# Winograd convolution with batch norm: storing the transformed input point by point, splitting the last pair's copies, and moving the first weights forward

## The chip, the cores and the metric

The kernel runs on one core of one Trainium2 chip. The metric is device time in microseconds of one execution, taken as the median of several runs. Beside it stands one profiled execution, whose trace gives the start and the duration of every instruction on TensorE (PE; its weight loads are PEld), VectorE (DVE), ScalarE (ACT), GpSimd (POOL) and SyncE (SP, which here issues most of the DMAs).

## The reference

```python
# x (2, 2048, 1024), w (3, 1024, 1024), mean, var, g, b (1024,), all bfloat16
xp = jnp.pad(x, ((0, 0), (1, 1), (0, 0)))
y = sum(jnp.einsum('bsc,cd->bsd', xp[:, k:k + S, :], w[k]) for k in range(3))
y = (y - mean) * (g / jnp.sqrt(var + 1e-5)) + b
return silu(y)
```

It is a convolution of three taps along the sequence, over 1024 channels in and out, followed by batch norm with given statistics and SiLU.

## The kernel before, in words

The convolution is done in the Winograd manner: six output rows (R = 6) at a time are made from eight "points" (NJ = 8). The input is transformed to eight points, the weights are transformed to eight points, the two are multiplied point by point, and the eight products are combined into six output rows. A sequence of 2048 rows gives NB = 342 groups of six.

**Input transform.** The rows of a batch are loaded in 17 overlapping windows: 16 of 128 rows (256 KB, 21 groups each) and a last one of 33 rows (6 groups). `load_x` (L125) issues each on SP's queue, into 12 rotating buffers. A matrix `rm` (128 rows by 8 points by 21 groups, built on VectorE, L79 to L104) does the transform: for each of eight channel tiles, one matmul (L278) with a piece of the window as the stationary operand and `rm` as the moving one writes 168 columns into PSUM. Window 0 uses a shifted copy of the matrix, `rm0`, made by `first_matrix`. Windows are taken in pairs, and a pair is done in three jobs (`t_jobs`, `t_job`): a has channel tiles 0 to 2, b has 3 to 5, c has 6 and 7. A job has its matmuls for the first window of the pair, then for the second, into two neighbouring PSUM banks, and is then copied in one instruction to `T_sb` in SBUF, as bf16: 1008 values per partition for a and b, 672 for c. The 33-row window is one job of 384 values. `T_sb` lies as channel tile, point, group.

Each copy goes to ScalarE (L289) or VectorE (L291). The choice is made when the program is built: `ends` and `busy` keep a rough clock for both engines, and a copy is given to the one that would finish first. Once built, the order on every engine is fixed.

**Weights.** The first weights (128 output channels of w, three chunks of 256 KB, one for each tap) are loaded between the windows; `W0_AT` says after which. `prepare_first` makes six of their eight points: `even_part` and `transform_w` run on GpSimd (L169, L179, L190), and use two multiples of taps that ScalarE makes, four times tap 2 (L175) and twice tap 1 (`double_w`, L157). Points 0 and 7 are taps as loaded.

**Products.** A `Unit` is one batch by 128 output channels, in four PSUM banks. `product` makes eight matmuls (L324) of 342 columns, one per channel tile. Products come for points 1, 3, 2, 4, 5, 6, and later 7 and 0. Points 1 and 2 are summed in bank 3 of the unit, points 3 and 4 in bank 0, points 5 and 6 in bank 2. Copies of the intermediate sums go to ScalarE (`copy`, L335 and L337), and the combinations to VectorE (`combine`, L342). After the third product (point 2), ScalarE copies bank 3 into `sd[:, 0]`, and VectorE makes `sd[:, 1]` of bank 3 and an earlier copy; this is called the sd copy and the sd pass below. The rows end in SiLU on ScalarE (L347).

**What is laid into what.** All jobs of batch 0 run first (`ahead`), in PSUM banks 0 to 7. The 25 jobs of batch 1, numbered 0 (the 33-row window) to 24 below, are laid between the matmuls of the first unit: `Between` is called after every matmul of a product, and issues jobs so that jobs 0 to 22 are spread over the first 32 matmuls (products of points 1, 3, 2 and 4). They use the bank pairs 4-5, 6-7 and 1-2 in turn, so a job waits for the copy of the job three before it. The product of point 5 then takes bank 2, and has to wait for the copy of job 20. Jobs 23 and 24 follow that product. After that there are only products, to the end.

Of the kernel before, what the change touches and what calls it, by code (L numbers as in the profile page):

```python
# [15 lines left out]
P = 128  # L16
R = 6
NJ = 8
W0_AT = (5, 8, 11)
W0_USE = 16  # L20
EARLY = 23
XBUFS = 12
WARM = 6
WT = 21

@with_exitstack
def kernel(
# [51 lines left out]
    def transform_matrix():  # L79
        v = nc.vector  # L80
        val = consts.tile([P, 3, WT], I32, name="val")
        nc.gpsimd.iota(val, pattern=[[1, 3], [-R, WT]], base=-1, channel_multiplier=1)
        m = consts.tile([P, 4, 3, WT], FP32, name="m")
        f = consts.tile([P, 3, 2, WT], FP32, name="f")
        c = consts.tile([P, 2, WT], FP32, name="c")
        rm = consts.tile([P, NJ, WT], BF16, name="rm")
        m0, m2, m4, m6 = (m[:, q] for q in range(4))
        for q, coef in ((1, -8.0), (2, 1.0), (3, 1.0), (0, 36.0)):
            v.tensor_scalar(m[:, q], val, float(2 * q), coef, op0=ALU.is_equal, op1=ALU.mult)
        for k, (c4, c6) in enumerate(((34.0, -8.0), (40.0, -32.0), (10.0, -2.0))):  # L90
            v.scalar_tensor_tensor(out=f[:, k], in0=m4[:, 1:3], scalar=c4, in1=m2[:, 1:3], op0=ALU.mult, op1=ALU.add)
        v.scalar_tensor_tensor(out=c, in0=m6[:, 0:2], scalar=-36.0, in1=m0[:, 0:2], op0=ALU.mult, op1=ALU.add)
        for k, (c4, c6) in enumerate(((34.0, -8.0), (40.0, -32.0), (10.0, -2.0))):
            v.scalar_tensor_tensor(out=f[:, k], in0=m6[:, 1:3], scalar=c6, in1=f[:, k], op0=ALU.mult, op1=ALU.add)
        v.scalar_tensor_tensor(out=c, in0=m4[:, 0:2], scalar=189.0, in1=c, op0=ALU.mult, op1=ALU.add)
        f1, f2, f3 = (f[:, k] for k in range(3))
        for j, a0, s0, a1, op in (
            (1, f1[:, 0], 1.0, f1[:, 1], ALU.add), (2, f1[:, 0], 1.0, f1[:, 1], ALU.subtract),
            (3, f2[:, 1], 2.0, f2[:, 0], ALU.add), (4, f2[:, 1], -2.0, f2[:, 0], ALU.add),
            (5, f3[:, 0], 2.0, f3[:, 1], ALU.add), (6, f3[:, 0], 2.0, f3[:, 1], ALU.subtract),  # L100
            (0, m2[:, 1], 23.625, c[:, 1], ALU.add), (7, m2[:, 0], -23.625, c[:, 0], ALU.subtract),
        ):
            v.scalar_tensor_tensor(out=rm[:, j], in0=a0, scalar=s0, in1=a1, op0=ALU.mult, op1=op)
        return rm  # L104

    rm = transform_matrix()
# [8 lines left out]
    def busy(e, size):  # L115
        clock[e] = ends(e, size)

    order = [NW - 1] + list(range(2, NW - 1)) + [0, 1]
    xwin = {}

    def load_x(bi, wi):
# [38 lines left out]
            eng.tensor_scalar(t, raw[dc][:, 1], 2.0, 0.0, op0=ALU.mult, op1=ALU.add)  # L160
        double[dc] = t

    def even_part(dc, q, eng, by=None):

        w0, w2 = raw[dc][:, 0], raw[dc][:, 2]
        e = epool.tile([P, CT, P], FP32, name=f"e{q}")
        f, h = (w2, w0) if q == 1 else (w0, w2)
        if q == 0:
            eng.tensor_tensor(e, w0, w2, op=ALU.add)  # L169
        elif eng is nc.vector:  # L170
            eng.scalar_tensor_tensor(out=e, in0=f, scalar=4.0, in1=h, op0=ALU.mult, op1=ALU.add)  # L171
        else:
            t = spool.tile([P, CT, P], BF16, name="w1x2")
            if by is nc.scalar:
                by.mul(t, f, 4.0)  # L175
                busy("act", CT * P)
            else:
                by.tensor_scalar(t, f, 4.0, 0.0, op0=ALU.mult, op1=ALU.add)
            eng.tensor_tensor(e, t, h, op=ALU.add)  # L179
        if eng is nc.vector:  # L180
            busy("dve", CT * P)
        sums[dc, q] = e
# [22 lines left out]
        act_work.append(lambda: double_w(dc, nc.scalar))  # L205
        dve_work.extend((second, third))

    def prepare_first(dc):

        even_part(dc, 0, nc.gpsimd)  # L210
        transform_w(dc, 0, (0,))
        even_part(dc, 1, nc.gpsimd, nc.scalar)
# [4 lines left out]
        even_part(dc, 2, nc.gpsimd, nc.gpsimd)  # L217
        transform_w(dc, 2)

    prm = consts.tile([P, 4, DC], BF16, name="prm")  # L220
# [7 lines left out]

    def first_matrix():

        v = ps[0:P - 1, 1, 256:256 + NJ * WT]
        nc.tensor.matmul(v, lhsT=ident[:, 1:P], rhs=rm.rearrange("p j n -> p (j n)"), start=True, stop=True)
        nc.scalar.copy(rm0[0:P - 1].rearrange("p j n -> p (j n)"), v)

    def params():

        v = ps[:, 1].bitcast(BF16)[:, 0:4 * DC]
# [15 lines left out]
    def t_jobs(bi):  # L253


        i = 0
        while i < NW:
            two = order[i:i + 2] if order[i] < NW - 1 else order[i:i + 1]
            i += len(two)
            n = LAST if two[0] == NW - 1 else WT  # L260
            wins = [
                (*xwin[bi, wi], rm if wi else rm0, min(P, S - (R * WT * wi - 1)) if wi else P - 1) for wi in two
            ]
            c0 = 0
            while c0 < CT:
                nct = min(512 // (NJ * n), CT - c0)
                yield wins, T_sb[bi][:, c0:c0 + nct, :, two[0] * WT:two[0] * WT + len(two) * n], n, c0, nct
                c0 += nct

    def t_job(job, bank):  # L270
        wins, dst, n, c0, nct = job
        nb, size = len(wins), nct * NJ * n
        clock["pe"] = max(clock["pe"], wins[-1][1], bank_free.get(bank, 0.0))
        src = ps[:, bank:bank + nb, 0:size]
        v = src.rearrange("p b (c j n) -> p b c j n", j=NJ, n=n)
        for q, (xw, _, mat, rows) in enumerate(wins):
            for c in range(nct):
                nc.tensor.matmul(  # L278
                    v[:, q, c], lhsT=xw[0:rows, (c0 + c) * P:(c0 + c + 1) * P], rhs=mat[0:rows, :, 0:n],
                    start=True, stop=True,  # L280
                )
        dst = dst.rearrange("p c j (b n) -> p (c j) b n", b=nb)
        src = src.rearrange("p b (q n) -> p q b n", n=n)
        clock["pe"] += nb * size / 2.3
        e = min(("act", "dve"), key=lambda k: ends(k, nb * size))
        busy(e, nb * size)
        bank_free[bank] = clock[e] + 100.0
        if e == "act":
            nc.scalar.copy(dst, src)  # L289
        else:  # L290
            nc.vector.tensor_copy(dst, src)  # L291

    NK = -(-NB // P)
    NBP = NK * P
# [5 lines left out]
    class Unit:  # L300
# [15 lines left out]
        def product(self, q, j, add, between):  # L316
            dc = self.dc
            nsl = slice(self.lo, self.hi)
            for ct in range(CT):
                if j == 0 or j == NJ - 1:  # L320
                    lhsT = raw[dc][:, 0 if j == 0 else 2, ct]
                else:
                    lhsT = wts[dc, (j - 1) // 2][:, (j - 1) % 2, ct]
                nc.tensor.matmul(  # L324
                    self.bank[q], lhsT=lhsT, rhs=T_sb[self.bi][:, ct, j, nsl],
                    start=not add and ct == 0, stop=ct == CT - 1, skip_group_check=add,
                )
                clock["pe"] += (self.hi - self.lo) / 2.35
                between()
# [149 lines left out]
    for i, wi in enumerate(order):  # L479
        load_x(0, wi)  # L480
        if i in W0_AT:
            load_w(0, (0, 2, 1)[W0_AT.index(i)], 0)

    def ahead(jobs, job_n):
        for job in jobs:
            t_job(job, job_n % 4 * 2)
            if job_n == 0:
                first_matrix()
            if job_n == 2:
                params()  # L490
            if job_n == 5:
                scales()
            if job_n == W0_USE:
                prepare_first(0)
            job_n += 1

    ahead(t_jobs(0), 0)
    for wi in order:
        load_x(1, wi)
    for k in (0, 2, 1):  # L500
        load_w(0, k, 1)
# [1 line left out]
    class Between:  # L503


        n = done = cols = 0
        jobs = list(t_jobs(1))
        size = [len(wins) * nct * n for wins, _, n, _, nct in jobs]

        def do(self):  # L510
# [85 lines left out]
```

## Time and profile before

| | us |
|---|---|
| Median of 3 runs | 190.70 |
| Lowest and highest run | 190.54, 190.92 |
| Profiled execution, its own time | 190.48 |
| Span of its trace, first to last instruction | 188.7 |
| TensorE busy in the span | 177.2 (94%) |
| VectorE, ScalarE, GpSimd busy | 155.5, 111.1, 137.4 |

The 1.78 us between the profiled time and the span lie outside the trace. A row of the timeline reads: start, length, engine, line, operation, output and input by name, shape, count, and in brackets the idle time of the engine before it and what ended it. The chain of waits is followed back from the last instruction: each piece is what the next one waited for.

### The profile page before, as it was taken

How to read it: one execution, taken by the hardware profiler on the slowest of the kernel's cores; microseconds unless marked ns; L12 is line 12 of the kernel's file. 1: busy time of each engine (PE TensorE's matmuls, PEld its weight loads, DVE VectorE, ACT ScalarE, POOL GpSimd, SP SyncE). 2: the span in 40 equal slices, each digit the busy share in tenths (PEclk: the TensorE clock that was granted, in tenths of full speed). 3: DMA queues.
4: the chain of work that ended last, by engine and by line, in shares of the span. 5: the costliest groups of instructions: out<-in, count | busy, mean ns of one | idle time of the engine just before them, and what ended most of it. 6: DMA issues, size and time to landing. Idle time of an engine off the chain costs nothing.

```text
span 188.7 us, 3725 instructions
## 1 busy us (share of the span) xinstructions
PE 177.2 (94%) x1404; PEld 124.5 (66%) x1404; DVE 155.5 (82%) x214; ACT 111.1 (59%) x181; POOL 137.4 (73%) x79
## 2 busy tenths in 40 slices
PE   7677799999999999999999999999999999999990
PEld 2455688776666666666666666666666666668980
DVE  5546888889989899988898899879979996769680
ACT  4777887875456565365645554555455555454780
POOL 3535999976797889999999999699999872000032
PEclk9999999999999999999999999999999999999999
DMA  5999999066244938499669586998596676976756
GB/s 160 333 316 368 375 364 228 5 186 154 47 78 31 205 70 171 129 236 207 115 128 194 112 166 181 195 197 155 116 205 115 125 116 124 182 137 118 149 109 119
DMA packets 86908, 31.72 MB, mean 168 GB/s; under 512 B 73502, under 2 KB 82728, under 8 KB 86890
## 3 DMA queue, kind: packets, MB, share of 16 engines
q1 hardware_dynamic: 85994, 31.28, 74.0%
q10 hardware_dynamic: 768, 0.18, 0.5%
q8 instruction: 11, 0.18, 0.4%
q0 software_dynamic: 128, 0.02, 0.1%
q14 instruction: 7, 0.06, 0.1%
HBM read 14.82 MB, written 8.39 MB: 123 GB/s over the span
## 4 chain that ended last, share of the span: by engine, by line
PE 84%; DMA 8%; DVE 4%; issue 1%; POOL 0%; POOLq 0%; SPq 0%; DVEq 0%
PE ps L324 78%; DMA xw<-in_x_dram 8%; PE ps L278 5%; DVE T_sb L291 4%; PE ps L429 1%; POOL out_dram L446 0%; POOLq L591 0%; DVE o L430 0%; SPq L125 0%; DVEq L291 0%
## 5 line engine op out<-in xcount | busy, mean ns | idle before, releaser
L324 PE MATMUL ps<-T_sb,u 128*128 128x342 bf16 (+2 forms) x816 | 120.9, 299 | 0.2 <-ACT T_sb L289 0.2
L324 PEld LDWEIGHTS <-u 128*128 128x128 bf16 x816 | 76.8, 97 | 33.4 <-issue 0.2
L190 POOL TENSOR_TENSOR u<-e,w1x 128x1024 bf16<-128x1024 f32 x32 | 70.4, 2222 | 9.4 <-DVE e L171 9.2
L324 PE MATMUL ps<-T_sb,wch 128*128 128x342 bf16 (+2 forms) x272 | 42.4, 299 | 0.0
L347 ACT ACTIVATE yT<-ps,beta,scale 128x342 bf16<-128x342 f32 (+5 forms) x51 | 34.1, 704 | 11.8 <-PE ps L324 11.8
L342 DVE SCALAR_TENSOR_TENSOR t<-ps,sd 128x684 f32<-128x684 f32 (+2 forms) x51 | 39.1, 821 | 0.6
L190 POOL TENSOR_TENSOR u<-e,wch 128x1024 bf16<-128x1024 f32 x16 | 36.6, 2309 | 1.7 <-DMA wch<-in_w_dram 1.2
L324 PEld LDWEIGHTS <-wch 128*128 128x128 bf16 x272 | 25.7, 97 | 11.5
L335 ACT COPY pc<-ps 128x342 f32<-128x342 f32 (+2 forms) x34 | 14.5, 426 | 31.7 <-PE ps L324 30.9
L291 DVE CAST T_sb<-ps 128x1008 bf16<-128x1008 f32 (+2 forms) x20 | 21.6, 1104 | 10.9 <-PE ps L278 10.7
L278 PE MATMUL ps<-rm,xw 128*128 128x168 bf16 (+2 forms) x272 | 25.5, 233 | 5.2 <-DMA xw<-in_x_dram 4.5
L289 ACT CAST T_sb<-ps 128x1008 bf16<-128x1008 f32 (+2 forms) x30 | 25.1, 874 | 6.8 <-PE ps L278 6.8
L342 DVE SCALAR_TENSOR_TENSOR ps<-ps,t 128x684 f32<-128x684 f32 (+2 forms) x34 | 28.3, 832 | 0.6
L171 DVE SCALAR_TENSOR_TENSOR e<-wch 128x1024 f32<-128x1024 bf16 x14 | 28.6, 2046 | 0.0
L278 PEld LDWEIGHTS <-xw 128*128 128x128 bf16 (+2 forms) x272 | 20.1, 98 | 11.3 <-DMA xw<-in_x_dram 6.6
L342 DVE SCALAR_TENSOR_TENSOR ps<-ps,pc 128x342 f32<-128x342 f32 (+2 forms) x34 | 16.9, 497 | 8.8 <-PE ps L324 5.7
L169 POOL TENSOR_TENSOR e<-wch 128x1024 f32<-128x1024 bf16 x8 | 19.0, 2372 | 4.5 <-DMA wch<-in_w_dram 2.9
L446 POOL DMA_DIRECT2D out_dram<-o x2 | 1.4, 710 | 25.6 <-ACT o L430 22.9
L347 ACT ACTIVATE yT<-t,beta,scale 128x684 bf16<-128x684 f32 (+2 forms) x17 | 15.7, 926 | 0.0
L342 DVE SCALAR_TENSOR_TENSOR t<-ps,t 128x684 f32<-128x684 f32 (+2 forms) x17 | 13.9, 818 | 0.0
L335 ACT COPY sd<-ps 128x342 f32<-128x342 f32 (+2 forms) x17 | 7.3, 430 | 10.1 <-PE ps L324 9.7
L337 ACT ACTIVATE pc<-ps 128x342 f32<-128x342 f32 (+2 forms) x17 | 7.5, 441 | 9.8 <-PE ps L324 6.0
(44 smaller groups left out, 47.2 us busy)
## 6 DMA issues: line engine op xcount, KB each, us to landing
xw<-in_x_dram SPq DMA_DIRECT2D x32, 256.0 KB
out_dram<-o SPq DMA_DIRECT2D x28, 192.0 KB
wch<-in_w_dram SPq DMA_DIRECT2D x9, 512.0 KB
out_dram<-o SPq DMA_DIRECT2D x14, 120.0 KB
wch<-in_w_dram SPq DMA_DIRECT2D x6, 256.0 KB
out_dram<-o SPq DMA_DIRECT2D x3, 128.0 KB
out_dram<-o SPq DMA_DIRECT2D x4, 64.0 KB
o<-yT SPq DMA_TRANSPOSE x15
```

The costliest lines, as they stand in the source:

```text
L169: eng.tensor_tensor(e, w0, w2, op=ALU.add)
L171: eng.scalar_tensor_tensor(out=e, in0=f, scalar=4.0, in1=h, op0=ALU.mult, op1=ALU.add)
L190: nc.gpsimd.tensor_tensor(wts[dc, q][:, i], sums[dc, q], o, op=(ALU.add, ALU.subtract)[i])
L278: nc.tensor.matmul(v[:, q, c], lhsT=xw[0:rows, (c0 + c) * P:(c0 + c + 1) * P], rhs=mat[0:rows, :, 0:n], start=True, stop=True,)
L289: nc.scalar.copy(dst, src)
L291: nc.vector.tensor_copy(dst, src)
L324: nc.tensor.matmul(self.bank[q], lhsT=lhsT, rhs=T_sb[self.bi][:, ct, j, nsl], start=not add and ct == 0, stop=ct == CT - 1, skip_group_che ...
L335: nc.scalar.copy(dst, self.bank[q])
L337: nc.scalar.mul(dst, self.bank[q], by)
L342: nc.vector.scalar_tensor_tensor(out=out, in0=in0, scalar=scalar, in1=in1, op0=ALU.mult, op1=op1)
L347: nc.scalar.activation(self.yT[:, rows, self.lo:self.hi], src, ACT.Silu, bias=beta[:, dc:dc + 1], scale=scale[:, dc:dc + 1])
L429: nc.tensor.transpose(v[:, a, q], self.yT[:, i, k * P:k * P + n], ident)
```

## The change

- `T_sb` is stored as point, channel tile, group, with the points in the order 1, 3, 2, 4, 5, 6, 0, 7 (`POS`); the transform matrix has its points in the same order.
- In batch 0 the 33-row window is no longer first; windows load and run as 2 to 15, 0, 33 rows, 1. The last pair (0, 1) uses banks 4-5, 6-7 and 1-2; the matmuls of window 0 of all three of its jobs come first, then the 33-row job, then the matmuls of window 1. After these each job's first two points are copied (`FRONT` = 2), and the other six points are copied after the first matmul of the first unit.
- Batch 1's jobs begin after the fifth matmul of the first unit (`SKIP` = 5), and are spread over the other 27.
- The three first weight chunks are issued after windows 4, 7 and 10 of the list instead of 6, 9 and 12. Four times tap 2 is made on ScalarE behind job 9 of batch 0, and `prepare_first` comes behind job 14 instead of job 16.
- `first_matrix` and `params` come together ahead of job 3, in bank 6, instead of behind jobs 0 and 2 in bank 1.
- The six bf16 matmuls on zeros ahead of the first window become two in fp32; the zeros are fp32 too.

The diff, cut to its core:

```diff
-W0_AT = (5, 8, 11)
-W0_USE = 16
+W0_AT = (3, 6, 9)
+W0_USE = (9, 14)
+SKIP = 5
+POS = {j: q for q, j in enumerate((1, 3, 2, 4, 5, 6, 0, 7))}
+FRONT = 2
-WARM = 6
+WARM = 2
-    T_sb = [tpool.tile([P, CT, NJ, NB], BF16, name=f"T_sb{bi}") for bi in range(B)]
+    T_sb = [tpool.tile([P, NJ, CT, NB], BF16, name=f"T_sb{bi}") for bi in range(B)]
-    zeros = consts.tile([P, 512], BF16, name="zeros")
+    zeros = consts.tile([P, 512], FP32, name="zeros")
-    order = [NW - 1] + list(range(2, NW - 1)) + [0, 1]
+    full = list(range(2, NW - 1)) + [0, 1]
+    order = [full[:-1] + [NW - 1] + full[-1:], [NW - 1] + full]
...
+    def t_copy(job, bank, pos=slice(0, NJ)):
+        wins, dst, n, c0, nct = job
+        nb = len(wins)
+        src = ps[:, bank:bank + nb, 0:nct * NJ * n]
+        size = nb * nct * (pos.stop - pos.start) * n
+        dst = dst[:, pos].rearrange("p j c (b n) -> p c j b n", b=nb)
+        src = src.rearrange("p b (c j n) -> p c j b n", j=NJ, n=n)[:, :, pos]
+        e = min(("act", "dve"), key=lambda k: ends(k, size))
...
+    pairs = [full[q:q + 2] for q in range(0, len(full), 2)]
+    for job_n, job in enumerate(t_jobs(0, pairs[:-1])):
+        if job_n == 3:
+            first_matrix()
+            params()
+        if job_n == 7:
+            scales()
+        t_job(job, job_n % 4 * 2)
+        if job_n == W0_USE[0]:
+            four = times_four(0, 1, nc.scalar)
+        if job_n == W0_USE[1]:
+            prepare_first(0, four)
+    ends_0 = list(zip(t_jobs(0, pairs[-1:]), (4, 6, 1)))
+    for job, bank in ends_0:
+        t_products(job, bank, (0,))
+    for job in t_jobs(0, [[NW - 1]]):
+        t_job(job, 0)
+    for job, bank in ends_0:
+        t_products(job, bank, (1,))
+        t_copy(job, bank, slice(0, FRONT))
...
         def __call__(self):
             self.n += 1
-            while self.done < EARLY and self.cols * 4 * CT < min(self.n, 4 * CT) * sum(self.size[:EARLY]):
+            if self.n == 1:
+                for job, bank in ends_0:
+                    t_copy(job, bank, slice(FRONT, NJ))
+            part = min(self.n, 4 * CT) - SKIP
+            while self.done < EARLY and self.cols * (4 * CT - SKIP) < part * sum(self.size[:EARLY]):
                 self.do()
```

What the built program's order shows beside this: in the stage of batch 1's jobs the copies now go to VectorE and ScalarE in strict turn up to job 15 (even jobs to VectorE), then jobs 16, 18, 20, 22 to ScalarE and 17, 19, 21 to VectorE. On VectorE the sd pass now stands ahead of the copy of job 17; before, it stood behind it. On ScalarE the sd copy stands behind the copy of job 16 in both. Of the last two whole pairs of batch 0, VectorE copies (12,13)a, (12,13)c and (14,15)b.

More of the change, by code (lines that the diff above doesn't have):

```diff
@@ L102, in transform_matrix @@
         ):
-            v.scalar_tensor_tensor(out=rm[:, j], in0=a0, scalar=s0, in1=a1, op0=ALU.mult, op1=op)
+            v.scalar_tensor_tensor(out=rm[:, POS[j]], in0=a0, scalar=s0, in1=a1, op0=ALU.mult, op1=op)
         return rm
@@ L161, in double_w, with times_four, even_part @@
         double[dc] = t
-    def even_part(dc, q, eng, by=None):
+    def times_four(dc, q, eng):
+        f = raw[dc][:, 2 if q == 1 else 0]
+        t = spool.tile([P, CT, P], BF16, name="w1x2")
+        if eng is nc.scalar:
+            nc.scalar.mul(t, f, 4.0)
+            busy("act", CT * P)
+        else:
+            eng.tensor_scalar(t, f, 4.0, 0.0, op0=ALU.mult, op1=ALU.add)
+        return t
+    def even_part(dc, q, eng, four=None):
         w0, w2 = raw[dc][:, 0], raw[dc][:, 2]
@@ L172, in even_part @@
         else:
[L173 to L179, printed above, removed]
+            eng.tensor_tensor(e, four, h, op=ALU.add)
         if eng is nc.vector:
@@ L206, in prepare_w, with prepare_first @@
         dve_work.extend((second, third))
-    def prepare_first(dc):
+    def prepare_first(dc, four):
         even_part(dc, 0, nc.gpsimd)
         transform_w(dc, 0, (0,))
-        even_part(dc, 1, nc.gpsimd, nc.scalar)
+        even_part(dc, 1, nc.gpsimd, four)
         double_w(dc, nc.scalar)
@@ L216, in prepare_first @@
         transform_w(dc, 1, (1,))
-        even_part(dc, 2, nc.gpsimd, nc.gpsimd)
+        even_part(dc, 2, nc.gpsimd, times_four(dc, 2, nc.gpsimd))
         transform_w(dc, 2)
@@ L229, in first_matrix @@
     def first_matrix():
-        v = ps[0:P - 1, 1, 256:256 + NJ * WT]
+        v = ps[0:P - 1, 6, 256:256 + NJ * WT]
         nc.tensor.matmul(v, lhsT=ident[:, 1:P], rhs=rm.rearrange("p j n -> p (j n)"), start=True, stop=True)
@@ L235, in params @@
     def params():
-        v = ps[:, 1].bitcast(BF16)[:, 0:4 * DC]
+        v = ps[:, 6].bitcast(BF16)[:, 0:4 * DC]
         nc.tensor.transpose(v, rows, ident[0:4 * DC, 0:4 * DC])
@@ L251, in scales, with windows, t_jobs, t_products @@
         nc.gpsimd.tensor_scalar(scale, sc, 1.0 / 36.0, 0.0, op0=ALU.mult, op1=ALU.add)
[L253 to L259, printed above, removed]
-            n = LAST if two[0] == NW - 1 else WT
[L261 to L265, printed above, removed]
-                nct = min(512 // (NJ * n), CT - c0)
[L267 to L276, printed above, removed]
+    def windows(bi, two):
+        return [(*xwin[bi, wi], rm if wi else rm0, min(P, S - (R * WT * wi - 1)) if wi else P - 1) for wi in two]
+    def t_jobs(bi, groups):
+        for two in groups:
+            n = LAST if two[0] == NW - 1 else WT
+            for c0 in range(0, CT, 512 // (NJ * n)):
+                nct = min(512 // (NJ * n), CT - c0)
+                dst = T_sb[bi][:, :, c0:c0 + nct, two[0] * WT:two[0] * WT + len(two) * n]
+                yield windows(bi, two), dst, n, c0, nct
+    def t_products(job, bank, which):
+        wins, _, n, c0, nct = job
+        v = ps[:, bank:bank + len(wins), 0:nct * NJ * n].rearrange("p b (c j n) -> p b c j n", j=NJ, n=n)
+        for q in which:
+            xw, landed, mat, rows = wins[q]
+            clock["pe"] = max(clock["pe"], landed, bank_free.get(bank, 0.0)) + nct * NJ * n / 2.3
             for c in range(nct):
@@ L281, in t_job @@
                 )
[L282 to L286, printed above, removed]
+    def t_copy(job, bank, pos=slice(0, NJ)):
[6 more added lines that the diff above has]
+        e = min(("act", "dve"), key=lambda k: ends(k, size))
+        busy(e, size)
         bank_free[bank] = clock[e] + 100.0
@@ L291, in t_job @@
             nc.vector.tensor_copy(dst, src)
+    def t_job(job, bank):
+        t_products(job, bank, range(len(job[0])))
+        t_copy(job, bank)
     NK = -(-NB // P)
@@ L324, in product @@
                 nc.tensor.matmul(
-                    self.bank[q], lhsT=lhsT, rhs=T_sb[self.bi][:, ct, j, nsl],
+                    self.bank[q], lhsT=lhsT, rhs=T_sb[self.bi][:, POS[j], ct, nsl],
                     start=not add and ct == 0, stop=ct == CT - 1, skip_group_check=add,
@@ L477, in store @@
             )
-    for i, wi in enumerate(order):
+    for i, wi in enumerate(order[0]):
         load_x(0, wi)
@@ L482 @@
             load_w(0, (0, 2, 1)[W0_AT.index(i)], 0)
[L484 to L498, printed above, removed]
+    pairs = [full[q:q + 2] for q in range(0, len(full), 2)]
[18 more added lines that the diff above has]
+        t_copy(job, bank, slice(0, FRONT))
+    for wi in order[1]:
         load_x(1, wi)
@@ L506 @@
         n = done = cols = 0
-        jobs = list(t_jobs(1))
+        jobs = list(t_jobs(1, [[NW - 1]] + pairs))
         size = [len(wins) * nct * n for wins, _, n, _, nct in jobs]
```

## The prediction

> **What bounds the kernel now.** I read the chain of waits first, as shares and then in order of time.
>
> ```profile
> PE 84%; DMA 8%; DVE 4%; issue 1%; POOL 0%; POOLq 0%; SPq 0%; DVEq 0%
> ...
> 9.70 6.44 DMA xw<-in_x_dram
> ...
> 18.24 3.87 DVE T_sb L291 x4
> ...
> 38.31 137.22 PE ps L324 x960
> ```
>
> There are three stages. To 16.1 us the loading of x sets the end. Then come copies out of PSUM and the mix of batch 1's jobs with the first unit. From 38.3 us TensorE issues products without a gap until the tail. Nothing in the change touches that last stage, so the question is only when it starts. I take as its mark the first matmul of the product of point 5, at 36.25: the chain of waits goes over to TensorE alone there, but for jobs 23 and 24. The second view is the timeline of TensorE around the change of stage.
>
> ```profile
> 16.18 2.64 PE L278 MATMUL ps<-rm,xw 128*128 128x168 bf16 x29 [1.24 <-DMA xw<-in_x_dram]
> 19.14 0.38 PE L278 MATMUL ps<-rm,xw 127*128 127x168 bf16 x3 [0.31 <-DVE T_sb L291]
> 19.75 1.39 PE L278 MATMUL ps<-rm,xw 128*128 128x168 bf16 x13 [0.23 <-DMA xw<-in_x_dram]
> 21.35 0.30 PE L324 MATMUL ps<-T_sb,u 128*128 128x342 bf16 x1 [0.21 <-ACT T_sb L289]
> 22.15 0.59 PE L278 MATMUL ps<-rm,xw 128*128 128x168 bf16 x6 [0.17 <-DVE T_sb L291]
> ```
>
> Window 13 lets TensorE go at 16.18, window 1 at 19.75; the first product starts at 21.35, and job 1 at 22.15. The third view is VectorE and ScalarE where the product of point 2 ends, and one later unit.
>
> ```profile
> 32.29 1.00 ACT L289 CAST T_sb<-ps 128x1008 bf16<-128x1008 f32 x1 [0.16 <-PE ps L278]
> 33.09 1.21 DVE L291 CAST T_sb<-ps 128x1008 bf16<-128x1008 f32 x1 [0.59 <-PE ps L278]
> 33.19 0.45 ACT L335 COPY sd<-ps 128x342 f32<-128x342 f32 x1
> 34.21 0.50 DVE L342 SCALAR_TENSOR_TENSOR sd<-pc,ps 128x342 f32<-128x342 f32 x1
> ...
> 52.80 0.51 DVE L342 SCALAR_TENSOR_TENSOR sd<-pc,ps 128x342 f32<-128x342 f32 x1 [0.35 <-ACT sd L335]
> ```
>
> The copies of jobs 16 (ScalarE, 32.29) and 17 (VectorE, 33.09) run side by side; the sd pass comes behind job 17's copy and finds the sd copy done at 33.64. In the later unit it waits for that copy. The groups by shape give the prices: a copy of 1008 values 1.207 on VectorE and 1.002 on ScalarE, of 672 0.853 and 0.726, of 384 0.558 and 0.484; the next one starts 0.08 and 0.10 before the end of the last. The trace spaces L278 matmuls 0.0725 apart and L324 0.145. From the last matmul of a job to its copy 0.27 pass on ScalarE and 0.34 on VectorE (where it has two waits), and from a copy's end to a waiting matmul 0.05.
>
> **The loading.** Bytes ahead of window 1 stay the same. Window 13 has 0.26 of a window less before it (33 of 128 rows). Windows land 0.68 apart there (16.14, 16.82, 17.50, 18.16), so it lands 0.18 sooner; if SP's first issue slot is also saved (six issues take 2.77), 0.46 more at most is one slot, so I bound the gain by 0.18 and 0.48 and take 0.30. The weights' three issues move ahead of two windows each on SP; bytes and issues (0.43 each) are the same, and GpSimd's work starts sooner, which no TensorE wait in the trace asks for.
>
> **The head of batch 0.** Two fp32 matmuls on zeros take between one and four times a bf16 one each; the bf16 ones stand 0.43 apart, so 0.9 to 3.4 in all, after a memset twice as long (0.27 more). TensorE is free between 2.3 and 4.9, against 3.86. Job 3 must wait for ScalarE to copy `rm0` and `prm` out of bank 6 (0.30 and 0.19): about 8.0 instead of 7.19. Both are hidden by the wait of 1.14 that the timeline has at 9.66; without it they would cost up to 0.8. Four times tap 2 and twice tap 1 (1.06 and 1.05, at 17.5 and 18.5 before) fall into ScalarE's gaps at about 13.3 and 15.7; their chunks land before that, and the copies of (10,11) and (12,13) queued behind them are not held up. The new layout copies the same runs of 42 values; the 384-value copy has runs of 6 and lies on the same slope as the others, so I take stride as free.
>
> **The tail of batch 0.** Times here are less the 0.30. VectorE has (12,13)a from 16.61 (the first copy followed window 13 by 0.43), then (12,13)c and (14,15)b back to back: 16.61 + 1.13 + 0.77 + 1.21 = 19.72. Bank 6 waits for that copy, so window 0's matmuls for job b start at 19.77. Five matmuls (0.36) and the 33-row job (0.24) stand before window 1, which therefore starts at 20.37, well after its landing. Three matmuls, 0.34, and a copy of 252 values (0.42 on VectorE's slope) give 21.28, and the first product starts at 21.40 with its weight load behind the wait; less 0.30, 21.10, against 21.35. So the wait for ScalarE becomes one for VectorE. Six matmuls of the unit take 0.87, job 0 0.24: job 1 starts at 22.21, against 22.15. The gain is five product matmuls already done. The back copies (756 values: 0.95 and 0.80) lie beside the six matmuls. Split copies cost 0.42 + 0.95 - 1.21 = 0.16 more each.
>
> **Batch 1's jobs.** Before, jobs 1 to 15 took 22.15 to 31.67: 80 matmuls (5.80), 21 products (3.05) and 0.7 of waits for banks. After, there are 18 products (2.61), so TensorE alone needs 8.41. But a bank's turn with VectorE is 0.36 + 0.34 + 1.21 + 0.05 = 1.96 and with ScalarE 1.69, and three jobs with their 3.6 products are only 1.68 of TensorE. Followed job by job with the prices above, the turn's average of 1.83 and the queues leave 0.86 of waits: 9.27. Job 16 starts at 31.48, against 31.67. Of 0.73 that five products are worth, 0.2 remains.
>
> **The sd pass.** Now it stands on VectorE ahead of job 17's copy, and waits for the sd copy, which stands on ScalarE behind job 16's copy. With job 16 at t: its copy t + 0.68 to 1.68, the sd copy to 2.03, the sd pass from 2.08 (0.50), job 17's copy 2.50 to 3.70, job 20 (same banks) at 3.76, its copy on ScalarE 4.39 to 5.39, and the product of point 5 at t + 5.46. Before it was 36.25 - 31.67 = 4.58. So 0.88 is lost. Queued behind the pass are the copies of jobs 17, 19 and 21, and TensorE waits for 17 and 19.
>
> **The sum.** 31.48 + 5.46 = 36.94, 0.69 later than 36.25; with the bounds of the landing, 0.5 to 0.8. On the profiled run's 190.48 this is 191.17. The median lies 0.22 above that run, so I forecast 191.4. About 0.2% (0.38 us) is what a measurement of this kernel can tell from no change.
>
> [...]
>
> **The rivals.**
> *The pass costs nothing:* the sd copy gets ahead, or the pass does not wait. Then job 17's copy starts at t + 1.6 as before, point 5 comes about 4.65 after 31.48, at 36.1, and the time is 190.6: no change. For it: 33.09 shows that VectorE was free then. Against: the row at 52.80.
> *Faster:* the landing, not VectorE, ends the tail. If (14,15)b is copied before window 1 lands (18.88 for 15 of its 16 parts, less 0.30), the first product starts at about 19.6, 1.5 sooner than in my sum, and all behind it: 36.94 - 1.5 = 35.4, 0.8 sooner than before, 189.9. It decides when the copy that frees bank 6 ends before 18.6. Against: three VectorE copies from 16.3 sum to 3.1.
> *Later still:* one part of window 1 landed at 19.71, 0.8 after the others, behind a 16 KB instruction load that took 1.1 from 17.48. If such a load falls later, window 1 may come up to 1 us after 20.1: 192.2.
>
> **How the numbers follow.** My forecast 0.63, no cost of the pass 0.19, the faster rival 0.13, later still 0.05. The range 190.4 to 191.8 holds the first two with their bounds and leaves out 0.18; the likeliest case alone has 191.2 to 191.5. Slower by over 0.2% takes the forecast and the last rival, 0.68; within 0.2%, 0.19; faster, 0.13.
>
> **What would show it.** In the profile after: first product near 21.1 with job 1 near 22.2; VectorE idle by about 1 us ahead of the sd pass, ended by ScalarE's sd copy; a wait of about 1 us of TensorE on VectorE's copy at job 20; point 5 near 36.9. I am wrong if that idle time is missing, if the first product starts before 20.5, or if banks stop making TensorE wait from 22 to 31.

## The result, and the profile after

The changed kernel takes 193.03 us (median of 6 runs, 192.46 to 193.25) against 190.62 us (6 runs of the kernel before beside it, 190.28 to 191.03): a ratio of 1.0133, 95% interval 1.0114 to 1.0151 (the two medians alone give 1.0126). The forecast was 191.4, and its range ended at 191.8. The direction was right; the size was 1.6 us short.

The profiled execution took 193.03, with a span of 191.2 (before: 190.48 and 188.7). First the chain of waits of the changed kernel, in order of time (start, length, what).

```profile
15.88 0.41 PE ps L282 x3
16.31 1.97 DVE T_sb L301 x2
18.30 1.22 DVE T_sb L301
19.56 1.40 PE ps L282 x19
20.98 0.38 ACT T_sb L299
...
32.00 1.63 ACT T_sb L299 x2
33.63 0.35 ACT sd L349
...
34.00 0.51 DVE sd L356
34.52 1.13 DVE T_sb L301
...
39.45 138.79 PE ps L338 x960
```

Two things are to be seen. From 15.88 to 35.68 the chain runs as the prediction told it: VectorE's three copies, the rest of window 0 and window 1 behind them, and later ScalarE's copy of job 16, the sd copy, the sd pass, and job 17's copy behind the pass. And the last line has 138.79 us for the same 960 matmuls that took 137.22 before. The prediction had nothing there.

The timeline of TensorE at the same places (in brackets the idle time before the row and what ended it):

```profile
15.88 1.33 PE L282 MATMUL ps<-rm,xw 128*128 128x168 bf16 x16 [0.28 <-DMA xw<-in_x_dram]
19.56 1.53 PE L282 MATMUL ps<-rm,xw 127*128 127x168 bf16 x21 [0.27 <-DVE T_sb L301]
21.40 1.04 PE L338 MATMUL ps<-T_sb,u 128*128 128x342 bf16 x6 [0.31 <-ACT T_sb L299]
35.68 0.59 PE L282 MATMUL ps<-rm,xw 128*128 128x168 bf16 x6 [0.89 <-DVE T_sb L301]
```

Window 13 lets TensorE go at 15.88, 0.30 sooner, as forecast. The first product starts at 21.40 (forecast 21.10), six of its matmuls run at once, and at 35.68 TensorE has waited 0.89 for VectorE's copy ahead of job 20. The bracket at 21.40, and the chain at 20.98, name ScalarE's copy (job b of the last pair, to 21.35), where the forecast had VectorE's (job a, to 21.25). That is only the one that ended last: in e8 below the first product starts at 21.76, 0.15 behind VectorE's copy as here, while ScalarE's still runs to 21.78. So VectorE's copy held it, as forecast. VectorE and ScalarE at job 16:

```profile
32.00 1.63 ACT L299 CAST T_sb<-ps 128x672 bf16<-128x672 f32 x2 [0.16 <-PE ps L282]
33.51 0.46 ACT L349 COPY sd<-ps 128x342 f32<-128x342 f32 x1
34.00 0.51 DVE L356 SCALAR_TENSOR_TENSOR sd<-pc,ps 128x342 f32<-128x342 f32 x1 [1.16 <-ACT sd L349]
34.43 3.25 DVE L301 CAST T_sb<-ps 128x1008 bf16<-128x1008 f32 x3
```

VectorE stands idle for 1.16 ahead of the sd pass, ended by the sd copy: the sign that the prediction named. The first matmul of point 5 starts at 37.38, 1.13 later than the 36.25 of before (forecast 0.69). So the span's 2.5 us are 1.13 up to point 5, 1.57 in the 960 matmuls (138.79 - 137.22), and 0.2 back in the tail (from the end of that piece to the end of the span 12.96, before 13.17).

The second part is seen in the groups by line, and in successive products of the timeline, first before:

```profile
L324 PE MATMUL ps<-T_sb,u 128*128 128x342 bf16 (+2 forms) x816 | 120.9, 299 | 0.2 <-ACT T_sb L289 0.2
L324 PE MATMUL ps<-T_sb,wch 128*128 128x342 bf16 (+2 forms) x272 | 42.4, 299 | 0.0
```

```profile
46.28 1.32 PE L324 MATMUL ps<-T_sb,u 128*128 128x342 bf16 x8
47.44 1.32 PE L324 MATMUL ps<-T_sb,wch 128*128 128x342 bf16 x8
```

and after:

```profile
L338 PE MATMUL ps<-T_sb,u 128*128 128x342 bf16 (+2 forms) x816 | 121.9, 300 | 0.3 <-ACT T_sb L299 0.3
L338 PE MATMUL ps<-T_sb,wch 128*128 128x342 bf16 (+2 forms) x272 | 42.9, 300 | 0.0
```

```profile
46.34 1.33 PE L338 MATMUL ps<-T_sb,wch 128*128 128x342 bf16 x8
47.52 1.34 PE L338 MATMUL ps<-T_sb,u 128*128 128x342 bf16 x8
48.69 1.34 PE L338 MATMUL ps<-T_sb,wch 128*128 128x342 bf16 x8
```

Neither weights nor waits differ by kind: products with raw weights (wch) and with transformed ones (u) are both longer, and no idle time stands in brackets. Eight matmuls take 47.44 - 46.28 = 1.16 before and (48.69 - 46.34) / 2 = 1.175 after, from start to start. The mean start-to-start of neighbouring 342-column matmuls in the trace is 145.15 ns before (934 intervals) and 146.87 ns after (935). After, it goes by the channel tile, the same for all points, units and both batches: tiles 0 and 4 take 144.0 to 144.5 ns, tiles 1, 2, 3, 5, 6 and 7 take 147 to 149. What is peculiar to tiles 0 and 4 in the new layout is that their rows begin on a multiple of 16 bytes, counted from the start of T_sb, which lies on one (at bytes 21984 and 65760 for the two batches in the program as built): a row has 342 values of 2 bytes, tile ct begins at 684 x ct, and 684 = 42 x 16 + 12. In the layout before, 5472 bytes lay between the rows of successive matmuls (342 x 16); in the new one they lie side by side.

### The profile page after: what moved, and what is told of

Same layout as the page of the kernel before. It is cut to its first block, busy times and chain, and to the rows that moved or that the text cites. A ratio compares the mean times of both kernels' runs of the same rounds, so it can differ in the third digit from the quotient of the medians.

```text
span 191.2 us, 3728 instructions
## 1 busy us (share of the span) xinstructions
PE 179.2 (94%) x1402; PEld 125.6 (66%) x1402; DVE 158.8 (83%) x217; ACT 110.5 (58%) x181; POOL 137.4 (72%) x79
## 4 chain that ended last, share of the span: by engine, by line
PE 84%; DMA 7%; DVE 4%; ACT 1%; SPq 1%; issue 0%; POOL 0%; POOLq 0%; DVEq 0%
PE ps L338 78%; DMA xw<-in_x_dram 7%; PE ps L282 5%; DVE T_sb L301 4%; ACT T_sb L299 1%; PE ps L443 1%; SPq L130 1%; POOL out_dram L460 0%; DVE sd L356 0%; POOLq L616 0%; DVE o L444 0%; ACT sd L349 0%; DVEq L301 0%
## 5 line engine op out<-in xcount | busy, mean ns | idle before, releaser
L338 PE MATMUL ps<-T_sb,wch 128*128 128x342 bf16 (+2 forms) x272 | 42.9, 300 | 0.0
L199 POOL TENSOR_TENSOR u<-e,wch 128x1024 bf16<-128x1024 f32 x16 | 37.6, 2368 | 1.7 <-DMA wch<-in_w_dram 1.1
L301 DVE CAST T_sb<-ps 128x1008 bf16<-128x1008 f32 (+5 forms) x23 | 22.8, 1017 | 9.7 <-PE ps L282 9.5
L186 DVE SCALAR_TENSOR_TENSOR e<-wch 128x1024 f32<-128x1024 bf16 x14 | 30.7, 2192 | 0.0
L299 ACT CAST T_sb<-ps 128x1008 bf16<-128x1008 f32 (+5 forms) x30 | 24.6, 854 | 8.4 <-PE ps L282 7.8
L282 PE MATMUL ps<-rm,xw 128*128 128x168 bf16 (+2 forms) x272 | 24.8, 233 | 4.5 <-DMA xw<-in_x_dram 2.1
L184 POOL TENSOR_TENSOR e<-wch 128x1024 f32<-128x1024 bf16 x8 | 18.0, 2249 | 3.6 <-PE ps L338 2.0
L356 DVE SCALAR_TENSOR_TENSOR sd<-pc,ps 128x342 f32<-128x342 f32 (+2 forms) x17 | 8.2, 485 | 6.4 <-ACT sd L349 6.4
```

What stands on the lines that cost most here:

```text
L199: nc.gpsimd.tensor_tensor(wts[dc, q][:, i], sums[dc, q], o, op=(ALU.add, ALU.subtract)[i])
L282: nc.tensor.matmul(v[:, q, c], lhsT=xw[0:rows, (c0 + c) * P:(c0 + c + 1) * P], rhs=mat[0:rows, :, 0:n], start=True, stop=True,)
L338: nc.tensor.matmul(self.bank[q], lhsT=lhsT, rhs=T_sb[self.bi][:, POS[j], ct, nsl], start=not add and ct == 0, stop=ct == CT - 1, skip_grou ...
L356: nc.vector.scalar_tensor_tensor(out=out, in0=in0, scalar=scalar, in1=in1, op0=ALU.mult, op1=op1)
```

## The experiments

All times are ratios to the kernel before, run beside them on the same chip, with a 95% interval. "Point 5" is the start of the first matmul of the product of point 5; it and the start of the first product are read from the one profiled execution of each kernel.

### Which part of the change slows the products, and by what (e1 to e5)

**e1, the layout alone**, laid into the kernel before:

```diff
-    T_sb = [tpool.tile([P, CT, NJ, NB], BF16, ...
+    T_sb = [tpool.tile([P, NJ, CT, NB], BF16, ...
...
-                rhs=T_sb[self.bi][:, ct, j, nsl]
+                rhs=T_sb[self.bi][:, j, ct, nsl]
```

> The kernel before with one part of the change alone: T_sb is laid out point, channel tile, group (no new order of points, no split copies, nothing else). Layout theory: the start-to-start time of the 342-column product matmuls rises from 145.15 ns to about 146.9 ns; over some 900 of them that is +1.4 to +1.6 us, so about 192.1 us against 190.6, while point 5 still starts near 36.25. Rival (another part of the change, such as the fp32 zeros tile that shifts every later tile by 1 KB, slows the products): 145.15 ns and 190.6 us, no change.

Measured: 146.86 ns for each matmul, as the layout theory has it; 1.0178 (1.0158 to 1.0199). The rival is out. But the loss is 3.4 us where 1.5 was expected, and point 5 starts at 38.08 and not near 36.25, so the layout has another cost, taken up at e14.

**e2, the layout put back** in the changed kernel:

```diff
-    T_sb = [tpool.tile([P, NJ, CT, NB], BF16, ...
+    T_sb = [tpool.tile([P, CT, NJ, NB], BF16, ...
...
-                rhs=T_sb[self.bi][:, POS[j], ct, nsl]
+                rhs=T_sb[self.bi][:, ct, POS[j], nsl]
```

> The changed kernel with T_sb laid out channel tile, point, group as before, everything else of the change kept. Layout theory: product matmuls back to 145.1 to 145.2 ns, about -1.4 us against the changed kernel's 193.0: 191.5 to 191.7, that is +0.5% against before, with point 5 still near 37.4. Rival (another part slows the products): 146.9 ns and 193.0 us stay.

Measured: 145.15 ns to the digit, 137.21 us for the 960 matmuls, 1.0091 (1.0070 to 1.0113), point 5 at 37.60. The stage gave back 1.58 us; the ratio fell by 0.42%, 0.8 us. The ratios of this study scatter by some 0.3% around what the stages show, so stages are compared below where they can be.

**e3, rows padded** from 342 to 344 values in the changed kernel:

```diff
-    T_sb = [tpool.tile([P, NJ, CT, NB], BF16, ...
+    T_sb = [tpool.tile([P, NJ, CT, 344], BF16, ...
```

> The changed kernel with each row of T_sb padded from 342 to 344 values, so that every row starts on a 16-byte grid (688 = 43 x 16 bytes; the rows still follow one another in the order in which they are read). Grid theory (rows that start off 16 bytes are read more slowly; in the changed kernel only channel tiles 0 and 4 start on the grid, at 144.1 and 144.3 ns, the others take 147 to 149): all rows at about 144.2 ns, 2.7 ns x some 900 = 2.4 us less than the changed kernel: 190.5 to 190.8. Neighbour theory (it costs that successive matmuls read rows that lie side by side): 147 ns and 193.0 us stay.

The chain of waits of this kernel has for the stage of products:

```profile
39.57 137.07 PE ps L338 x960
```

Measured: 1.0039 (1.0025 to 1.0053), 1.72 us less in the stage than the changed kernel. It is not 144.2 ns for each, though: 929 of 935 intervals are 145 ns. So I read 145.0 as what such a matmul takes undisturbed, and the 144s of the other kernels as matmuls that made up time behind a long one. The mean of this run is 144.99.

**e4, another order of channel tiles**, the same rows at the same addresses:

```diff
-            for ct in range(CT):
+            for step in range(CT):
+                ct = step % 4 * 2 + step // 4
```

> The changed kernel with the eight channel tiles of each product taken in the order 0, 2, 4, 6, 1, 3, 5, 7: the same rows at the same addresses, but no two matmuls in a row read neighbours. Grid theory: tiles 0 and 4 at 144.2 ns, the other six at 147 to 148, 193.0 us as the changed kernel. Neighbour theory: near 145.2 ns for all, 1.4 to 1.5 us less: 191.5.

```profile
39.72 137.17 PE ps L339 x960
```

Measured: 145.10 ns, 1.0086 (1.0060 to 1.0111). One interval in eight is 148 ns or more (the fifth of each product), and the three behind it are 144.1 to 144.4. Six of eight rows still begin off the grid, and the mean is only 0.1 above 145.0: the grid alone is not the cause.

**e5, rows padded to 358 values**: 32 bytes between neighbours, the same remainders by 16 and 32 bytes as in the changed kernel, the same order.

> The changed kernel with each row of T_sb padded from 342 to 358 values: a gap of 32 bytes after every row, but the starts have the same remainders by 16 and by 32 bytes as in the changed kernel (716 = 684 + 32), and the rows are read in the same order. If what costs is that a row begins off the grid inside the 16 or 32 bytes in which the row just read ended, the gap removes it: 145.0 to 145.2 ns, some 1.5 us less than the changed kernel, 1.008 to 1.010 of before. If what costs is the run of remainders alone (0, 12, 8, 4 from matmul to matmul), 146.9 ns and 1.013 of before stay.

```profile
39.58 137.27 PE ps L338 x960
```

Measured: 145.21 ns, 1.0035 (1.0015 to 1.0054). Remainders alone are out as well. Tiles 1 and 5 still take 148.3 ns here, but the three behind each take 144.2. What the five runs leave is both together: the mean rises by 1.7 ns where rows begin off the 16-byte grid in the very piece in which the row just read ended. Take away either (e3 the grid, e4 and e5 the neighbour) and all but 0.2 ns goes. Single long matmuls are left even so, one in eight in e4 and two in eight in e5; there the ones behind make up the time, and in the changed kernel they do not. How is not shown. That the piece has 16 bytes I read from two more numbers: in the changed kernel the row of tile 2 begins 1368 bytes in, where a piece of 8 would begin, and takes 148.3; and in e3 every second row begins off a grid of 32, in the same 32 bytes in which the row before it ended, and takes 145.0. Why such starts cost time, no run here shows.

**e9, the kernel before with rows padded to 344 values.**

> The kernel before with each row of T_sb padded from 342 to 344 values and nothing of the change. In the kernel before no product reads neighbours in a row (5472 bytes lie between them), so by the neighbour reading only the small rest above 145.0 ns can go: 0.15 ns x some 940 = 0.14 us less, 0.999 of before. A reading by which starts off the 16-byte grid alone cost something would give more: six of eight rows are off the grid there, and at 2.7 ns each it would have to be 2 us less, 0.99.

Measured: 145.04 ns, 137.11 us in the stage (137.22 before), 0.9987 (0.9971 to 1.0003). That is the small rest and not 2 us: the layout before was already clear of the effect.

### The sd pass (e6, e12)

**e6, padded rows, and the first unit's sd pass issued behind the first matmul of the product of point 4**, so that job 17's copy stands ahead of it on VectorE:

```diff
-            self.combine(sd[:, 1], pa, 2.0, b3, ALU.subtract)
+            todo = [lambda: self.combine(sd[:, 1], pa, 2.0, b3, ALU.subtract)]
...
+            def then():
+                between()
+                if todo:
+                    todo.pop()()
-            self.product(0, 4, True, between)
+            self.product(0, 4, True, then)
```

> The changed kernel with rows padded to 344 values, and with the first unit's sd pass on VectorE put behind job 17's copy (it is issued after the first matmul of the product of point 4). Theory of the prediction: TensorE's wait of 0.89 us at job 20 goes, point 5 starts 0.8 to 0.9 us sooner than with the padding alone (37.53), at 36.6 to 36.7, and the time falls from 1.0039 of before to 0.999 to 1.000. Rival (job 17's copy was not what TensorE's chain hung on; the banks make it wait in another place): point 5 stays at 37.3 to 37.5, and 1.004.

VectorE's timeline, and the chain of waits behind it:

```profile
33.55 1.21 DVE L301 CAST T_sb<-ps 128x1008 bf16<-128x1008 f32 x1 [0.69 <-PE ps L282]
34.68 0.50 DVE L356 SCALAR_TENSOR_TENSOR sd<-pc,ps 128x342 f32<-128x342 f32 x1
35.45 1.21 DVE L301 CAST T_sb<-ps 128x1008 bf16<-128x1008 f32 x1 [0.27 <-PE ps L282]
```

```profile
34.82 0.60 PE ps L282 x6
35.45 1.22 DVE T_sb L301
36.71 1.32 PE ps L338 x8
```

Measured: 0.9999 (0.9979 to 1.0019); point 5 at 36.71, against 37.51 with the padding alone. Job 17's copy starts at 33.55 in place of 34.57 (e3), the 0.89 ahead of job 20 is gone, and point 5 comes 15.28 behind the first product in place of 15.96. From job 16 to point 5 4.74 pass in place of 5.43. The price of the pass, 0.7, is shown. It is not the whole 0.88, since a wait of 0.3 takes its place: point 5 writes bank 2, and job 20's copy, now on VectorE, frees it at 36.67. In e11 below that wait is half as long, and job 16 to point 5 takes 4.58, as in the kernel before.

**e12, the same with job 20's copy given to ScalarE** (VectorE's planned clock put 3 us ahead for that one choice).

> The kernel with padded rows and the sd pass behind job 17's copy, and with the copy of job 20 (banks 1 and 2; the product of point 5 writes bank 2) given to ScalarE in place of VectorE. In the kernel without this, point 5 waits 0.3 us for that copy (35.45 to 36.67). Theory: on ScalarE it ends by 36.3, point 5 starts at 36.4 in place of 36.71, and the time is 0.998 of before. Rival (ScalarE's queue, with copies back to back from 34.13 to 37.50, ends it no sooner): 36.7 or later, 1.000.

```profile
35.95 1.03 ACT T_sb L299
...
37.02 1.32 PE ps L338 x8
```

Measured: 1.0004 (0.9986 to 1.0022). The copy starts at 35.95 and point 5 comes 15.27 behind the first product: the rival was right, ScalarE's queue ends it no sooner.

### The tail and the head (e7, e8, e10, e11, e13)

**e7, the last pair copied whole ahead of the products** (padded rows; the copies of six points behind are gone):

```diff
-        t_copy(job, bank, slice(0, FRONT))
+        t_copy(job, bank)
```

> The changed kernel with rows padded to 344 values, and with all eight points of the last pair copied ahead in one copy for each job (no six points behind). The prediction's step for the tail: the first product waits for a copy of 1008 values (1.21 us on VectorE) in place of one of 252 (0.42), so it starts 0.6 to 0.8 us later than the 21.55 with the padding alone, at 22.1 to 22.4, and point 5 comes later by 0.3 to 0.8; 1.006 to 1.008 of before. Rival (the banks set the pace of batch 1's jobs, whatever is ready before): the first product moves, but point 5 stays within 0.2 us of 37.53, and 1.004.

Measured: 1.0092 (1.0061 to 1.0122), some 1.0 us more than with the split. The first product starts at 21.74, only 0.2 later; but from 21.5 to nearly 25 the granted clock of TensorE in the profile is 0.50, and point 5 starts at 39.10. So the split is worth its place in this layout, in this profile by another way than I had priced it: TensorE stood still for 1.10 ahead of 21.74, and the clock fell, as is shown for e1 at e14. How much of the 1.0 us is the clock in the other executions is not shown; this one has the lowest mean clock of the six (0.985, the others 0.992 to 0.995).

**e8, the first weights put back** (padded rows; `W0_AT` 5, 8, 11, multiples at job 16).

> The changed kernel with rows padded to 344 values, and with the first weights and their multiples put back to where they were (loads behind windows 5, 8 and 11 of the order, multiples at job 16). Prediction's step: nothing on TensorE waits for them, so point 5 stays within 0.1 us of 37.53, and 1.004 of before. Rival (ScalarE's multiples, 1.06 and 1.05 us, stand in the way of the copies in the tail of batch 0 now or then): point 5 moves by 0.3 to 1.0 us, later if the old place was the worse one.

Measured: 1.0043 (1.0025 to 1.0061), against 1.0039 without the edit. Point 5 is 0.2 later in the profile, because the first product is (21.76); between the two lie 15.97, as in e3 (15.96). No cost of the weights' place is shown in the time, as forecast. It is not far off the path, though: in e3's own chain of waits twice tap 1 on ScalarE stands for 0.95 (from 16.51) ahead of the last copies of batch 0.

**e10, the old warm-up** of six bf16 matmuls, beside padded rows and the late sd pass:

```diff
-WARM = 2
+WARM = 6
-    zeros = consts.tile([P, 512], FP32, name="zeros")
+    zeros = consts.tile([P, 512], BF16, name="zeros")
```

> The kernel with padded rows and the sd pass behind job 17's copy, and with the warm-up put back to six bf16 matmuls on zeros (in place of two fp32 ones). Prediction's step: the head is hidden by the wait for x, so the first product stays within 0.1 us of 21.43, and 1.000 of before. Rival, from the chain of waits of the two padded kernels, which runs from the zeros through the fp32 matmuls (1.45 to 5.23) to ScalarE's rm and prm copies: the head is on the path, and without it the first product starts 0.2 to 0.5 us sooner, 0.998.

Measured: 0.9991 (0.9977 to 1.0006). The first product starts at 20.97, 0.46 sooner, which spoke for the rival. **e13** put it to the changed kernel alone:

> The changed kernel with one edit: the warm-up is six bf16 matmuls on zeros again in place of two fp32 ones. If the head's delay reaches the end of the stage through the release of the x buffers and the load that waits for it (10.30 in the changed kernel, 9.87 with the old warm-up and padding), window 13 lets TensorE go 0.3 to 0.4 us sooner than 15.88, the first product starts at 21.0 in place of 21.40 and point 5 at 37.0 in place of 37.38; 1.011 of before in place of 1.013. If the head is hidden (the prediction's step), point 5 stays at 37.4 and the ratio at 1.013.

```profile
21.51 1.04 PE ps L338 x6
```

Measured: the first product at 21.51 in place of 21.40, no gain; 1.0103 (1.0066 to 1.0139), an interval that holds 1.0133. The first product's start scatters from execution to execution: over the eight profiles with this tail and two fp32 matmuls it lies between 21.40 and 21.76 (mean 21.57), and over the three with the old warm-up (e10, e13, e15) at 20.97, 21.51 and 21.26 (mean 21.25). So the profiles lean towards a cost of the head of up to 0.3 us. The times do not show one (e13's interval holds 1.0133, and e15 is no faster than e11), and the question stays open.

**e11, SKIP = 0**, beside padded rows and the late sd pass: batch 1's jobs follow the first product matmul at once.

> The kernel with padded rows and the sd pass behind job 17's copy, and with SKIP = 0: batch 1's jobs start behind the first product matmul and not five matmuls later. Prediction's step: batch 1's jobs are paced by the turns of three pairs of banks, so five products done ahead are worth only 0.2 of their 0.73 us; job 16 moves by less than 0.3, point 5 stays at 36.4 to 36.9, 0.999 to 1.001. Rival (TensorE is the pace, the five matmuls are fully worth their time, or bank turns are entered later by them): point 5 moves by 0.5 to 0.7 us one way or the other.

```profile
21.42 0.30 PE L338 MATMUL ps<-T_sb,u 128*128 128x342 bf16 x1 [0.31 <-ACT T_sb L299]
22.15 0.91 PE L282 MATMUL ps<-rm,xw 33*128 33x48 bf16 x14 [0.42 <-ACT T_sb L299]
```

Measured: 0.9984 (0.9967 to 1.0000); point 5 comes 15.14 behind the first product, against 15.28 in e6. TensorE now waits 0.42 for the banks of the last pair at 22.15 where it had five matmuls to do, and still nothing is lost: job 1 comes 0.25 sooner behind the first product, the way from job 1 to job 16 takes 9.53 in place of 9.26, and from there to point 5 0.16 less. Five products done ahead were worth nothing, or a little less.

### What the layout costs beside the reading (e14), and the sum of the edits (e15)

**e14 is e1 with rows padded to 344 values.**

> The kernel before with T_sb laid out point by point (as in the run of the layout alone) and with rows padded to 344 values. Padding takes the reading's cost away (145.0 ns), 1.7 us. What is left above the kernel before should be the other cost that the layout alone showed: the first product waits for the last of the three copies of the last pair (22.00 in place of 21.35, then batch 1's jobs later and the clock in some runs at half): 1.005 to 1.010 of before with the first product at 21.9 to 22.3. Rival: the layout's only cost is the reading, and this is 0.999 to 1.001 with the first product at 21.35.

```profile
21.79 0.30 PE ps L324
...
39.14 0.73 ACT T_sb L289
39.92 136.12 PE ps L324 x952
```

Measured: 144.99 ns, 1.0047 (1.0017 to 1.0078), the first product at 21.79. So the layout alone has a second cost, 0.9 us by the ratio. Its cause is seen in part: in the program as built, the first product waits for the last copy of the last pair on both engines, where in the layout before it waited for the first of the three. That is 0.44 for the first product (21.79 against 21.35), but in this profile, the fastest of the 12 executions, only 0.2 at point 5 (36.45) and in the span (188.9). Four executions took 192.2 to 193.1, three of them with the lowest mean clocks of the 12 (0.987 to 0.989), so the rest may be the clock shown below; no trace shows one of these four. A copy of all eight points now reaches from the first point's rows to the last one's, and takes in rows that it does not write; that this is why the wait is set so wide is argued. e2 speaks for it in the other layout: its second matmul, of point 1, starts at 21.78, behind ScalarE's copy of the six other points (to 21.73). A like wait is at 39.92, ahead of the second unit. In e1 the wait had a consequence. TensorE's timeline, and its table by stretches (time, busy times of the engines, then the granted clock ahead of DMA share and GB/s), of e1:

```profile
19.52 1.38 PE L278 MATMUL ps<-rm,xw 128*128 128x168 bf16 x13 [0.25 <-DMA xw<-in_x_dram]
22.00 0.30 PE L324 MATMUL ps<-T_sb,u 128*128 128x342 bf16 x1 [1.10 <-DVE T_sb L291]
22.24 1.34 PE L278 MATMUL ps<-rm,xw 33*128 33x48 bf16 x14
```

```profile
21.00:22.00 1.00, 0.00 (x0) 0.03 (x1) 0.85 (x1) 0.68 (x2) 1.00 (x1) 1.00 1.05 385
22.00:23.00 1.00, 1.00 (x13) 0.79 (x14) 0.27 (x1) 0.00 (x0) 1.00 (x2) 0.78 1.03 377
23.00:24.00 1.00, 1.00 (x8) 0.73 (x6) 0.29 (x1) 0.39 (x1) 1.00 (x1) 0.50 1.06 389
24.00:25.00 1.00, 1.00 (x8) 0.93 (x7) 0.00 (x0) 0.61 (x1) 1.00 (x2) 0.50 1.07 393
25.00:26.00 1.00, 1.00 (x7) 0.80 (x6) 0.91 (x1) 0.13 (x1) 1.00 (x1) 0.51 0.92 336
```

After 1.10 us in which TensorE stood still the clock was halved from about 22.5 to 26. e7 has the same wait and the same fall, and in e14's profile a wait of 1.10 left the clock at 1.00. What makes the clock fall after one wait of 1.10 and not after another, no run here shows.

**e15, all four**: padded rows, late sd pass, old warm-up, SKIP = 0.

> The changed kernel with four edits together: rows padded to 344 values, the sd pass behind job 17's copy, the old warm-up, and SKIP = 0. If the single effects add (old warm-up 36.71 to 36.25, SKIP = 0 36.71 to 36.42), point 5 starts at 35.9 to 36.0, the products run at 145.0 ns, and the time is 0.996 to 0.998 of before, less than both kernels. If they do not add (the loads or VectorE's copies set the end of the tail either way), point 5 stays at 36.2 to 36.4, 0.998 to 0.999.

Measured: 1.0004 (0.9980 to 1.0028); first product at 21.26, point 5 15.14 behind it, at 36.40. The effects do not add: e10's gain does not come back beside e11's, whose 15.14 is in. Against 1.0133 the edits take the whole loss away, but no version here is shown to beat the kernel before; e11 and e9, at 0.9984 and 0.9987, come nearest, with intervals that reach 1.

## Why the prediction was wrong, point by point

**The loading: right.** Window 13 came 0.30 sooner, the value taken. That it fits to the digit is luck: in other profiles with the same order of loads it lets TensorE go between 15.53 (e7) and 16.09 (e12). It bought nothing that can be told from the scatter of the first product.

**The head and the weights: right** as far as the runs can tell. The two fp32 matmuls on zeros took 3.44 (from 1.45 to the 4.89 below), 1.72 each, four times the 0.43 of a bf16 one: the upper end of the forecast's range. The first window's matmuls start at 4.89 (forecast at most 4.9) and job 3 at 7.85 (forecast 8.0); that this stays hidden behind the loading is not contradicted by the times of e13 and e8, but a cost of up to 0.3 us is not excluded.

**The tail of batch 0: the way right, the size a little off.** VectorE's chain ended at 19.52 (forecast 19.42), the rest of window 0 and window 1 followed it, and VectorE's copy of job a let the first product go. That came at 21.40 and not 21.10, job 1 at 22.69 and not 22.21: five matmuls and the 33-row job ahead of window 1 took 0.78 and not 0.60, and the 33-row job of batch 1 0.32 and not 0.24. Job 1 is 0.48 later than forecast and point 5 0.44, so the whole miss at point 5 was made here. What the split prevents I had not seen at all: the wait of e1 and e14.

**Batch 1's jobs: right.** From job 1 to job 16 9.26, forecast 9.27. That five products done ahead are worth 0.2 was still too kind; e11 has them at nothing.

**The sd pass: right.** From job 16 (31.95) to point 5 5.43, forecast 5.46; e6 takes the pass out of the way and gets 0.7 back. The direction of the result was therefore no luck: the 1.13 at point 5 are of the kind forecast.

**The failed step** is "The new layout copies the same runs of 42 values", so "I take stride as free". For the writers that held: copies of 1008 values still take 1.21 on VectorE and 1.00 on ScalarE. But it prices the layout for the writers alone. The readers are 960 matmuls in a stage where TensorE is never idle, and I had said that nothing in the change touches that stage. A row there costs 1.72 ns more in the mean (146.87 - 145.15), 1.57 us in all. No rival had it either, so the range could not reach it.

The sum with the two terms put right: 191.17 + 0.44 (point 5 at 1.13 in place of 0.69) + 1.57 - 0.21 (tail) = 192.97, against 193.03 measured on the profiled run.

## What to carry to other kernels

When a buffer's layout changes, price it at its readers as well as its writers, above all where the readers are the stage that bounds the kernel: 2 ns in 145 are 1.6 us here, more than the wait of 0.89 for the copy behind the sd pass. Here rows that successive matmuls read side by side took 146.87 ns a matmul with most starts off a grid of 16 bytes, and 144.99 with all on it; two padding values in 342 did it (e3). And read the order on each engine for what stands ahead of a copy that frees a bank: VectorE stood idle 1.16 us ahead of the short sd pass, and job 17's copy waited behind it; with the pass behind that copy, point 5 came 0.7 us sooner (e6).

## What was not expected of the hardware

- Rows of 684 bytes, side by side and read in their order, take 146.87 ns for each 342-column matmul; with starts on 16 bytes 144.99, with another order 145.10, with 32 bytes between them 145.21.
- After 1.10 us without a matmul at 21 us of e1, and again in e7, the granted clock fell to 0.50 for some 3.5 us; the same wait in e14, and the wait of 1.24 us ahead of 16.18 in the kernel before, left it at 1.00.
- With the same head and tail the first product moved by up to 0.36 us between profiles (21.40 to 21.76), about as much as the smallest difference that a measurement of the whole kernel can tell (0.38).
